# First heads of an attention kernel: order of the loads, one head's hash bits apart, values and their scale later

## The chip, the cores and the metric

One core of a Trainium2 chip runs the kernel. The metric is device time in microseconds (us), the median of timed executions. A further execution was profiled; every duration below is from it.

## The reference

Two batches of 8 heads (16 heads, sequence 768, head size 64, fp32) go through attention with a hash mask: six projections of each q and k row give six sign bits, and a query sees a key only if all six agree. The result is the input of a top-1 mixture of experts (8 experts, 1536 tokens), whose output goes through a gated two-layer network.

```python
q_bits = (einsum('bhsd,dk->bhsk', q, proj) > 0)
k_bits = (einsum('bhsd,dk->bhsk', k, proj) > 0)
mask = q_bucket[:, :, :, None] == k_bucket[:, :, None, :]
scores = where(mask, q @ k.T / sqrt(D), -1e9)
attn = exp(scores - max(scores)) ; attn /= sum(attn) + 1e-9
x = attn @ v
out = moe2(moe(x))
```

## The kernel before, in words

**Operands of a head.** q and k of head h are loaded together as the tile `r` (128 x 768: 64 rows of q, 64 of k). `prep(h)` splits it into a high and a low part (`hi`, `lo`) and SyncE's queue (SP) moves the halves into four tiles of the head's set, `X`, `K2`, `K1`, `Y`: four moves of `hi`, two of `lo`, 192 KB each. `bits(g)` makes the sign bits of the four heads 4g to 4g+3: `dot(n, i)` is the projection of head i, half n, on TensorE into 32 rows of a PSUM tile, and `rows(n)` turns half n into +-0.5 on VectorE (tile `b`). `put_bits(h)` moves head h's 12 rows of q bits to `X` and of k bits to `K2` (two DMAs on SP). Head 0 gets its bits apart, straight into its set.

**Steps.** The attention is 96 steps k, six for each head. `scores(k)` (lines 402 and 403) is one block of 128 keys against 768 queries, followed by the exponential on ScalarE (line 404); `high(k)` and `low(k)` split it into two fp16 parts (ScalarE and GpSimd, lines 412 and 418); `pv` multiplies with the values, four steps later and two steps at a time. `mx(n)` (lines 385 and 388) computes the row maxima that are needed before the scores of a head: two matmuls and two VectorE reductions for each of its six query groups; after the sixth, `top` goes by a DMA into row 76 of the head's `X`. `mx` runs ahead of the steps: `mx(0)` to `mx(5)` come before step 0, and the list `AHEAD` (from `Q['ac']`) spreads the next: before the change `mx(6)`, `mx(7)` in step 2, `mx(8)` to `mx(11)` in step 3, then one in each step. `mx(12)`, the first of head 2, is in step 4, and needs head 2's bits in place.

**Order.** The order on each engine is the program order. `at(t, f)` and `spread(t, gen, d)` put a piece of work behind a time t in steps; `due(k - 0.5)` runs before step k's scores and `due(k)` at the end of step k. `Q` holds these times: `v4` and `vg0` for the value tiles of the first heads, `lr` and `lv` for loads, `vsd` for the scale, `hn` for the number of warming matmuls (`heat`, line 283: 512 columns of zeros, result unused) before step 0 and in steps 0 to 7.

**Values.** `load_v(g)` loads the values of four heads (768 KB), `vmax` takes their largest magnitude (four reductions), and `vscale(g)` turns that into a power of two: maxima, a transpose through PSUM (`psn`, line 531), a maximum of it (line 534), a broadcast matmul (`pso`, line 540), and a chain of small integer operations (lines 544 to 559) that ends with `sc`. `vsplit` and `vgate` (line 491: twelve matmul records from the tile `vt`) need `sc`. All of `psn`, `pso`, the bits of `bits(g)` without tiles of its own and `psg` of `vgate` come from `misc`, a PSUM pool with a single buffer; a new tile in it waits until the last reader of the one before it is done.

**Before the change** the loads of heads 0 to 3, the first values and the first `vt` are queued on SP at the start; the bits of heads 0 to 3 are made together, in two PSUM tiles of their own, two dots behind `mx(5)` and six behind the warming matmuls; `put_bits(1)` and `put_bits(2)` stand in the lead-in, as does most of `vscale(0)`.

Of the kernel before, what the change touches and what calls it, by code (L numbers as in the profile page):

```python
# [51 lines left out]
def moe_attention_kernel(ctx, tc, qk, v, vt, pj, wg, w1, w2, win, wout, out, cap):  # L52
# [8 lines left out]
    def f32(t):  # L61
        return t.bitcast(F32)

    def run(gen):
        for _ in gen:
            pass
# [191 lines left out]
                )  # L258


    Q = {'v': (-3.25, -4.75, -1.75, -2.25), 'vg': (-4.5, -4.75), 'vgd': 1, 'pr': (-13.0, -12.75, -12.0, -12.5), 'prd': 0.6, 'b0': 7.75, 'b': 1.75, 'bd': 0.5, 'vm0': (8.0, 8.25, 10.75, 13.0), 'vm': (-0.5, 4.75, 7.0, 12.25), 'vs': 13.25, 'pa': 1.5, 'ev': 0.5, 'lvt': -5.0, 'v4': (2.0, 3.75, 4.0, 16.25), 'vg0': (1.85, -4.4, 7.75), 'p2': 3.5, 'lr': (0, 3, 1.5, 4.5), 'lv': 5.5, 'vsd': 0.75, 'ac': (0, 0, 2, 6, 7, 8, 9, 10), 'hd': (3, 5, 17), 'hn': (4, 4, 2, 2, 4, 3, 0, 0, 0), 'ap': (0,), 'h0': (7,), 'hl': (4,), 'l0': (), 'll': (1, 10), 'ht': (5, 9)}


    with ExitStack() as actx:
# [81 lines left out]
        def signs(out, ps, c):  # L346
            dve.tensor_scalar(out=out, in0=ps, scalar1=0.0, scalar2=c, op0=ALU.is_gt, op1=ALU.subtract)

        def bits(g, tiles=None):

            b_t[g] = ph.tile([P, S], F32R, tag="b", name=f"b{g}", bufs=2)
            ps = [None] * 2

            def dot(n, i):
                if i == 0:
                    ps[n] = tiles[n] if tiles else misc(f"psb{g}{n}")
                c = slice(n * HS, (n + 1) * HS)
                pe.matmul(
                    ps[n][32 * i : 32 * i + 32, :HS], pj_sb[:, 0:32], rt[4 * g + i][:, c], start=True, stop=True
                )  # L360

            def rows(n):
                signs(b_t[g][:, n * HS : (n + 1) * HS], ps[n][:, :HS], cst_sb[:, 0:1])

            if tiles:
                for i in range(4):
                    for n in range(2):
                        dot(n, i)
                    yield
            for n in range(2):  # L370
                if not tiles:
                    for i in range(4):
                        dot(n, i)
                    yield
                rows(n)
                if not tiles:
                    yield

        def mx(n):
            h, c = divmod(n, NC)  # L380
            st = sets[h % 4]
            mm = mxs[h % 2]
            for n in range(2):
                ps = ps_m.tile([P, 512], F32, tag="m", name=f"psm{h}{c}{n}")
                pe.matmul(  # L385
                    ps[:, :HS], st["X"][0:76, c::NC], st["K2"][0:76, n * HS : (n + 1) * HS], start=True, stop=True
                )
                dve.tensor_reduce(out=mm[:, c, n : n + 1], in_=ps[:, :HS], axis=AX.X, op=ALU.max)  # L388
            if c == NC - 1:

                dve.tensor_reduce(out=top[:, h], in_=mm, axis=AX.X, op=ALU.max)
                sp.dma_start(out=f32(st["X"])[76:77, :].rearrange("o (p c) -> o p c", c=NC), in_=f32(top)[:, h])

        def scores(k):
            h, j = divmod(k, NC)
# [108 lines left out]
                )  # L504
                yield

        def load_v(g):
            vr_t[g] = pt.tile([P, 4, NC, D], F32, tag="vr", name=f"vr{g}")
            n = 4 * NC * D
            sp.dma_start(out=vr_t[g].rearrange("p h c d -> p (h c d)"), in_=v[:, g * n : (g + 1) * n])  # L510
            am_t[g] = ph.tile([P, 4], F32, tag="am", name=f"am{g}")

        def vmax(g, i):
# [136 lines left out]
        load_r(0)  # L650
        act.dma_start(out=pj_sb, in_=pj)
        dve.memset(wg_sb, 0.0)
        for h in range(1, 4):
            load_r(h)
        load_v(0)
        load_vt(0)
        for i in range(2):
            act.dma_start(out=wg_sb[i * D : (i + 1) * D, :, i], in_=wg[i * D : (i + 1) * D])
        st, r0 = sets[0], rt[0]
# [11 lines left out]
                signs(st[t][D : D + 12, c], ps[D : D + 12, :HS], cst_sb[D : D + 12, i : i + 1])  # L671
        run(pre[0])
        next(pre[1])
        for i in range(4):
            pool.dma_start(out=f32(sets[i]["K2"])[76:77], in_=neg)
        consts()
        pool.dma_start(out=xd[0:1, :], in_=zrow[:, :DM])
        DOT = (5,)
        b0 = bits(0, [ps_v.tile([P, 512], F32, tag="v", name=f"psb0{n}") for n in range(2)])
        for n in range(NC):  # L680
            mx(n)
            if n in DOT:
                next(b0)
        heat(ps_t, "t", Q["hn"][0])
        for i in range(4):
            vmax(0, i)
        vs = vscale(0)
        next(vs)
        next(vs)
        run(b0)  # L690
        next(vs)
        put_bits(1)
        run(pre[1])
        next(pre[2])
        put_bits(2)

        heat_t.clear()
        STEPS = NC * NH
# [26 lines left out]

            at(k, part, k)

        spread(0, vs, Q["vsd"])
        spread(Q["p2"], pre[2])
        for i in range(4):  # L730
            at(Q["lr"][i], load_r, 4 + i)
# [13 lines left out]
        for h in range(NH):  # L745
            k = NC * h + NC - 1 + LAG
            if h < NH - 1:
                at(k + Q["ev"], evac, h)
            if h % 2 == 0:
                if h == 0:  # L750
                    spread(Q["vg0"][0], vgate(0), Q["vg0"][1])
                else:
                    spread(Q["vg0"][2] if h == 2 else NC * h + Q["vg"][h % 4 // 2], vgate(h // 2), Q["vgd"])
            elif h < NH - 1:
                at(k + Q["pa"], pair, h // 2)
                at(NC * h + Q["lvt"], load_vt, h // 2 + 1)
        spread(66, route(0, lambda: misc("psr0")), 1.5)
        spread(84, weigh(0))
        spread(89, any_unmatched())
# [580 lines left out]
```

## Time and profile before

| | us |
|---|---|
| timed runs | 714.74, 714.94, 719.21 (median 714.94) |
| profiled execution | 712.88 |
| its span in the trace | 711.1 |

TensorE (PE) is busy for 682.9 us of the span, VectorE (DVE) 503.5, ScalarE (ACT) 376.8, GpSimd (POOL) 260.6. The page divides the span into 40 slices with busy shares and the granted TensorE clock; the mean clock over the span is 0.98. PEld is TensorE's weight load. Matmul records of neighbouring instructions overlap, so a step's length is read from starts, not from the sum of durations.

### The profile page before, as it was taken

How to read it: one execution, taken by the hardware profiler on the slowest of the kernel's cores; microseconds unless marked ns; L12 is line 12 of the kernel's file. 1: busy time of each engine (PE TensorE's matmuls, PEld its weight loads, DVE VectorE, ACT ScalarE, POOL GpSimd, SP SyncE). 2: the span in 40 equal slices, each digit the busy share in tenths (PEclk: the TensorE clock that was granted, in tenths of full speed). 3: DMA queues.
4: the chain of work that ended last, by engine and by line, in shares of the span. 5: the costliest groups of instructions: out<-in, count | busy, mean ns of one | idle time of the engine just before them, and what ended most of it. 6: DMA issues, size and time to landing. Idle time of an engine off the chain costs nothing. (4 is left out here: it accounts for less than half of the span.)

```text
span 711.1 us, 14232 instructions
## 1 busy us (share of the span) xinstructions
PE 682.9 (96%) x5528; PEld 598.2 (84%) x5528; DVE 503.5 (71%) x988; ACT 376.8 (53%) x713; POOL 260.6 (37%) x202
## 2 busy tenths in 40 slices
PE   7999999999998699999999998999999999999996
PEld 2689898898897489999999996788888888888885
DVE  6778889889999788778777785888888632222320
ACT  3468869778779366655666642333333442223420
POOL 4347877977982411110110001333333423311212
PEclk8789999999999999999999999999999999999999
DMA  7585855746480376666665543234333000000001
GB/s 224 120 227 130 239 141 156 226 127 167 98 230 25 115 238 223 218 208 209 209 213 189 193 150 123 89 128 137 121 119 118 1 17 29 30 16 1 0 30 59
DMA packets 37841, 94.14 MB, mean 132 GB/s; under 512 B 7576, under 2 KB 13720, under 8 KB 37760
## 3 DMA queue, kind: packets, MB, share of 16 engines
q1 hardware_dynamic: 34672, 85.71, 40.2%
q0 software_dynamic: 2400, 7.36, 3.1%
q8 instruction: 46, 0.75, 0.4%
q14 instruction: 35, 0.29, 0.1%
q10 hardware_dynamic: 688, 0.03, 0.1%
HBM read 67.14 MB, written 6.29 MB: 103 GB/s over the span
## 5 line engine op out<-in xcount | busy, mean ns | idle before, releaser
L418 POOL TENSOR_TENSOR plo<-pf,phi 128x768 f16<-128x768 f32 x86 | 146.7, 1728 | 60.6 <-ACT phi L412 25.9
L996 POOL TENSOR_TENSOR ib<-wi,ia 128x512 fp32r<-128x512 f32 x32 | 50.1, 1566 | 230.1 <-ACT ia L995 230.1
L388 DVE TENSOR_REDUCE mx<-psm 128x1 f32<-128x384 f32 x192 | 96.3, 548 | 20.1 <-PE psm L385 19.8
L404 ACT ACTIVATE pf<-pst 128x384 f32<-128x384 f32 x192 | 83.4, 486 | 48.9 <-PE pst L403 47.5
L135 DVE TENSOR_TENSOR wl<-raw,wh 128x512 fp32r<-128x512 f32 x128 | 86.7, 688 | 10.2 <-ACT wh L134 3.7
L1223 ACT ACTIVATE rl<-psg,b 128x512 f32<-128x512 f32 x64 | 37.3, 582 | 94.6 <-PE psg L1221 94.5
L1221 PE MATMUL psg<-yTh,ia 128*128 128x512 f32 (+1 forms) x256 | 86.4, 338 | 0.7 <-DVE rl L1224 0.2
L1224 DVE SCALAR_TENSOR_TENSOR rl<-rl,psg 128x512 f32<-128x512 f32 x64 | 35.1, 550 | 73.3 <-ACT rl L1223 73.3
L1221 PE MATMUL psg<-yTh,ib 128*128 128x512 f32 (+1 forms) x256 | 85.9, 335 | 0.0
L1221 PE MATMUL psg<-yTl,ia 128*128 128x512 f32 (+1 forms) x256 | 85.7, 335 | 0.0
L134 ACT ACTIVATE wh<-raw 128x512 fp32r<-128x512 f32 x128 | 77.3, 623 | 2.1 <-issue 1.5
L1243 PE MATMUL pso<-cl,gh 128*128 128x512 f32 x192 | 76.7, 399 | 0.5 <-POOL cl L996 0.5
L402 PE MATMUL pst<-Y,K 128*128 128x384 f32 x192 | 75.1, 391 | 2.0 <-ACT pf L404 2.0
L1243 PE MATMUL pso<-ch,gl 128*128 128x512 f32 x192 | 75.5, 393 | 0.0
L1243 PE MATMUL pso<-ch,gh 128*128 128x512 f32 x192 | 75.5, 393 | 0.0
L412 ACT ACTIVATE phi<-pf 128x768 f16<-128x768 f32 x85 | 71.7, 844 | 1.9
L978 PE MATMUL psy<-hh,wh 128*128 128x224 f32 x256 | 71.3, 279 | 0.0
L385 PE MATMUL psm<-K,X 76*128 76x384 f32 x192 | 66.8, 429 | 4.3 <-DVE mx L388 3.5
L978 PE MATMUL psy<-hl,wh 128*128 128x224 f32 x256 | 70.2, 274 | 0.0
L978 PE MATMUL psy<-hh,wl 128*128 128x224 f32 x256 | 70.1, 274 | 0.0
L403 PE MATMUL pst<-X,K 77*128 77x384 f32 x192 | 66.2, 345 | 0.0
L432 PE MATMUL psv<-vh,plo 128*128 128x73 f16 x576 | 63.6, 196 | 1.7 <-DVE plo L418 1.7
(204 smaller groups left out, 1642.6 us busy)
## 6 DMA issues: line engine op xcount, KB each, us to landing
raw<-in_w_dram SPq DMA_DIRECT2D x64, 512.0 KB
rc<-in_win_dram SPq DMA_DIRECT2D x16, 512.0 KB
rc<-in_wout_dram SPq DMA_DIRECT2D x16, 512.0 KB
r<-in_qk_dram SPq DMA_DIRECT2D x16, 384.0 KB
K<-hi SPq DMA_DIRECT2D x31, 192.0 KB
vr<-in_v_dram SPq DMA_DIRECT2D x4, 768.0 KB
vt<-in_vt_dram SPq DMA_DIRECT2D x8, 384.0 KB
Y<-hi SPq DMA_DIRECT2D x16, 192.0 KB
```

The costliest lines, as they stand in the source:

```text
L134: act.activation(wh[e, i][:, c], r, AF.Copy)
L135: lo.tensor_tensor(out=wl[e, i][:, c], in0=r, in1=f32(wh[e, i])[:, c], op=ALU.subtract)
L385: pe.matmul(ps[:, :HS], st["X"][0:76, c::NC], st["K2"][0:76, n * HS : (n + 1) * HS], start=True, stop=True)
L388: dve.tensor_reduce(out=mm[:, c, n : n + 1], in_=ps[:, :HS], axis=AX.X, op=ALU.max)
L402: pe.matmul(ps[:, :HS], st["K1"][:, kc], st["Y"][:, qc], start=True, stop=False)
L403: pe.matmul(ps[:, :HS], st["K2"][0:77, kc], st["X"][0:77, qc], start=False, stop=True)
L404: act.activation(pf.rearrange("k (c n p) -> k c n p", c=NC, n=2)[:, :, n], ps[:, :HS].rearrange("k (p c) -> k c p", c=NC), AF.Exp, scale=0 ...
L412: act.activation(phi_t[k], pf_t[k], AF.Copy)
L418: eng.tensor_tensor(out=plo_t[k], in0=pf_t.pop(k), in1=phi_t[k], op=ALU.subtract)
L978: pe.matmul(ps, l, r, start=n == 0, stop=n == 3 * KF - 1)
L1221: pe.matmul(ps, l, x, start=n == 0, stop=n == 3 * KD - 1)
L1243: pe.matmul(po[blk][s], l, r, start=first and n == 0, stop=last and n == 2)
```

## The change

- The lead-in loads only heads 0 and 1 at first. Head 2 is queued behind head 1's first moves, head 3 behind `put_bits(1)`, the first `vt` at the end of the lead-in. The first values go on ScalarE's queue behind `mx(5)` and behind `top` of head 0, which goes on that queue too.
- `bits` takes a list of heads. Head 1's bits are made alone behind `mx(5)`, and `put_bits(1)` follows. Heads 2 and 3 follow as `bits(0, [2, 3])` from time 1.25, spaced by 0.5, through `misc`; `put_bits(2)` stands at 3.5.
- `vscale(0)` stops behind its first maxima in the lead-in and goes on from time 1.0 in spaces of 0.5.
- The low part of head 1 is made by ScalarE and GpSimd, not by VectorE (`Q['ap']`).
- `mx(6)` to `mx(11)` come two in each of the steps 1, 2 and 3. Warming matmuls: 6 in the lead-in and 2, 2, 1, 1 in steps 0 to 3, in place of 4 and 4, 2, 2, 4, 3.
- The times of loads 4 to 7, of the second values, of `vsplit`, of `vgate(0)`, of `vmax(1)` and of the second `vt` are later by 0.25 to 3.75 steps.

```diff
--- before.py
+++ after.py
@@ -258,7 +258,7 @@
                 )
 
 
-    Q = {'v': (-3.25, -4.75, -1.75, -2.25), 'vg': (-4.5, -4.75), 'vgd': 1, 'pr': (-13.0, -12.75, -12.0, -12.5), 'prd': 0.6, 'b0': 7.75, 'b': 1.75, 'bd': 0.5, 'vm0': (8.0, 8.25, 10.75, 13.0), 'vm': (-0.5, 4.75, 7.0, 12.25), 'vs': 13.25, 'pa': 1.5, 'ev': 0.5, 'lvt': -5.0, 'v4': (2.0, 3.75, 4.0, 16.25), 'vg0': (1.85, -4.4, 7.75), 'p2': 3.5, 'lr': (0, 3, 1.5, 4.5), 'lv': 5.5, 'vsd': 0.75, 'ac': (0, 0, 2, 6, 7, 8, 9, 10), 'hd': (3, 5, 17), 'hn': (4, 4, 2, 2, 4, 3, 0, 0, 0), 'ap': (0,), 'h0': (7,), 'hl': (4,), 'l0': (), 'll': (1, 10), 'ht': (5, 9)}
+    Q = {'v': (-3.25, -4.75, -1.75, -2.25), 'vg': (-4.5, -4.75), 'vgd': 1, 'pr': (-13.0, -12.75, -12.0, -12.5), 'prd': 0.6, 'b0': 7.75, 'b': 1.75, 'bd': 0.5, 'vm0': (10.25, 11.0, 11.75, 13.0), 'vm': (-0.5, 4.75, 7.0, 12.25), 'vs': 13.25, 'pa': 1.5, 'ev': 0.5, 'lvt': -5.0, 'v4': (2.75, 3.75, 4.5, 16.25), 'vg0': (2.85, -4.4, 7.75), 'p2': 3.5, 'lr': (2, 3.5, 4.5, 5.5), 'lv': 6.5, 'vsd': 0.5, 'ac': (0, 2, 4, 6, 7, 8, 9, 10), 'hd': (3, 5, 17), 'hn': (6, 2, 2, 1, 1, 0, 0, 0, 0), 'ap': (0, 1), 'h0': (7,), 'hl': (4,), 'l0': (), 'll': (1, 10), 'ht': (5, 9)}
 
 
     with ExitStack() as actx:
@@ -346,13 +346,15 @@
         def signs(out, ps, c):
             dve.tensor_scalar(out=out, in0=ps, scalar1=0.0, scalar2=c, op0=ALU.is_gt, op1=ALU.subtract)
 
-        def bits(g, tiles=None):
-
-            b_t[g] = ph.tile([P, S], F32R, tag="b", name=f"b{g}", bufs=2)
+        def bits(g, heads=range(4), tiles=None):
+
+            if g not in b_t:
+                b_t[g] = ph.tile([P, S], F32R, tag="b", name=f"b{g}", bufs=2)
+            p = slice(32 * heads[0], 32 * heads[-1] + 32)
             ps = [None] * 2
 
             def dot(n, i):
-                if i == 0:
+                if i == heads[0]:
                     ps[n] = tiles[n] if tiles else misc(f"psb{g}{n}")
                 c = slice(n * HS, (n + 1) * HS)
                 pe.matmul(
@@ -360,21 +362,19 @@
                 )
 
             def rows(n):
-                signs(b_t[g][:, n * HS : (n + 1) * HS], ps[n][:, :HS], cst_sb[:, 0:1])
-
-            if tiles:
-                for i in range(4):
-                    for n in range(2):
-                        dot(n, i)
-                    yield
+                signs(b_t[g][p, n * HS : (n + 1) * HS], ps[n][p, :HS], cst_sb[p, 0:1])
+
             for n in range(2):
-                if not tiles:
-                    for i in range(4):
-                        dot(n, i)
-                    yield
-                rows(n)
+                for i in heads:
+                    dot(n, i)
                 if not tiles:
                     yield
+                    rows(n)
+                    yield
+            if tiles:
+                yield
+                rows(0)
+                rows(1)
 
         def mx(n):
             h, c = divmod(n, NC)
@@ -389,7 +389,7 @@
             if c == NC - 1:
 
                 dve.tensor_reduce(out=top[:, h], in_=mm, axis=AX.X, op=ALU.max)
-                sp.dma_start(out=f32(st["X"])[76:77, :].rearrange("o (p c) -> o p c", c=NC), in_=f32(top)[:, h])
+                (sp if h else act).dma_start(out=f32(st["X"])[76:77, :].rearrange("o (p c) -> o p c", c=NC), in_=f32(top)[:, h])
 
         def scores(k):
             h, j = divmod(k, NC)
@@ -504,10 +504,10 @@
                 )
                 yield
 
-        def load_v(g):
+        def load_v(g, eng=sp):
             vr_t[g] = pt.tile([P, 4, NC, D], F32, tag="vr", name=f"vr{g}")
             n = 4 * NC * D
-            sp.dma_start(out=vr_t[g].rearrange("p h c d -> p (h c d)"), in_=v[:, g * n : (g + 1) * n])
+            eng.dma_start(out=vr_t[g].rearrange("p h c d -> p (h c d)"), in_=v[:, g * n : (g + 1) * n])
             am_t[g] = ph.tile([P, 4], F32, tag="am", name=f"am{g}")
 
         def vmax(g, i):
@@ -650,10 +650,7 @@
         load_r(0)
         act.dma_start(out=pj_sb, in_=pj)
         dve.memset(wg_sb, 0.0)
-        for h in range(1, 4):
-            load_r(h)
-        load_v(0)
-        load_vt(0)
+        load_r(1)
         for i in range(2):
             act.dma_start(out=wg_sb[i * D : (i + 1) * D, :, i], in_=wg[i * D : (i + 1) * D])
         st, r0 = sets[0], rt[0]
@@ -671,28 +668,26 @@
                 signs(st[t][D : D + 12, c], ps[D : D + 12, :HS], cst_sb[D : D + 12, i : i + 1])
         run(pre[0])
         next(pre[1])
+        load_r(2)
         for i in range(4):
             pool.dma_start(out=f32(sets[i]["K2"])[76:77], in_=neg)
         consts()
         pool.dma_start(out=xd[0:1, :], in_=zrow[:, :DM])
-        DOT = (5,)
-        b0 = bits(0, [ps_v.tile([P, 512], F32, tag="v", name=f"psb0{n}") for n in range(2)])
+        b0 = bits(0, [1], [ps_v.tile([P, 512], F32, tag="v", name=f"psb0{n}") for n in range(2)])
         for n in range(NC):
             mx(n)
-            if n in DOT:
-                next(b0)
+        load_v(0, act)
+        run(b0)
+        put_bits(1)
+        load_r(3)
+        run(pre[1])
         heat(ps_t, "t", Q["hn"][0])
         for i in range(4):
             vmax(0, i)
         vs = vscale(0)
         next(vs)
-        next(vs)
-        run(b0)
-        next(vs)
-        put_bits(1)
-        run(pre[1])
         next(pre[2])
-        put_bits(2)
+        load_vt(0)
 
         heat_t.clear()
         STEPS = NC * NH
@@ -725,7 +720,9 @@
 
             at(k, part, k)
 
-        spread(0, vs, Q["vsd"])
+        spread(1.0, vs, Q["vsd"])
+        spread(1.25, bits(0, [2, 3]), 0.5)
+        at(3.5, put_bits, 2)
         spread(Q["p2"], pre[2])
         for i in range(4):
             at(Q["lr"][i], load_r, 4 + i)
@@ -753,7 +750,7 @@
                     spread(Q["vg0"][2] if h == 2 else NC * h + Q["vg"][h % 4 // 2], vgate(h // 2), Q["vgd"])
             elif h < NH - 1:
                 at(k + Q["pa"], pair, h // 2)
-                at(NC * h + Q["lvt"], load_vt, h // 2 + 1)
+                at(max(4.75, NC * h + Q["lvt"]), load_vt, h // 2 + 1)
         spread(66, route(0, lambda: misc("psr0")), 1.5)
         spread(84, weigh(0))
         spread(89, any_unmatched())
```

## Rows read from the trace of the kernel before

**Rows 1.** The page: busy time of each engine, share of the span, instructions.

```profile
PE 682.9 (96%) x5528; PEld 598.2 (84%) x5528; DVE 503.5 (71%) x988; ACT 376.8 (53%) x713; POOL 260.6 (37%) x202
```

**Rows 2.** Timeline of PE, first score record of steps 0, 2, 5 (both halves), 6, 95.

```profile
19.28 0.44 PE L402 MATMUL pst<-Y,K 128*128 128x384 f32 x1
...
22.65 0.45 PE L402 MATMUL pst<-Y,K 128*128 128x384 f32 x1
...
38.44 0.52 PE L402 MATMUL pst<-Y,K 128*128 128x384 f32 x1
39.08 0.52 PE L402 MATMUL pst<-Y,K 128*128 128x384 f32 x1
...
42.12 0.42 PE L402 MATMUL pst<-Y,K 128*128 128x384 f32 x1
...
231.18 0.45 PE L402 MATMUL pst<-Y,K 128*128 128x384 f32 x1 [0.62 <-ACT pf L404]
```

**Rows 3.** Stretches: length; busy PE, PEld, DVE, ACT, POOL; clock, DMA share, GB/s.

```profile
3.50:4.00 0.50, 0.00 (x0) 0.00 (x0) 0.07 (x1) 0.07 (x1) 0.00 (x0) 1.00 1.03 393
...
17.00:18.00 1.00, 1.00 (x7) 0.28 (x7) 0.00 (x0) 0.00 (x0) 0.00 (x0) 0.68 0.00 0
...
25.00:26.00 1.00, 0.00 (x0) 0.00 (x0) 0.96 (x5) 0.36 (x1) 0.58 (x1) 1.00 0.88 211
...
27.00:28.00 1.00, 1.00 (x7) 0.72 (x6) 0.88 (x2) 0.46 (x2) 0.93 (x1) 0.94 1.02 209
...
41.00:42.00 1.00, 1.00 (x27) 1.00 (x25) 1.00 (x4) 0.91 (x2) 0.00 (x0) 0.74 1.04 234
```

**Rows 4.** Timeline of PE, 13 to 40 us: dots, warming, maxima, gates.

```profile
13.27 2.77 PE L358 MATMUL psb<-r,pj_sb 128*32 128x384 f32 x4
...
15.97 1.84 PE L283 MATMUL heatt<-idle_sb 128*128 128x512 f16 x4
...
17.85 1.50 PE L358 MATMUL psb<-r,pj_sb 128*32 128x384 f32 x12
...
26.54 0.56 PE L385 MATMUL psm<-K,X 76*128 76x384 f32 x1 [1.63 <-DVE mx L388]
...
32.65 2.57 PE L491 MATMUL psg<-wg_sb,vt 128*128 128x16 f32 x12
```

**Rows 5.** Timeline of DVE and POOL, 14 to 28 us.

```profile
14.10 1.92 DVE L514 TENSOR_REDUCE am<-vr 128x1 f32<-128x384 f32 x4
...
19.44 1.14 DVE L347 TENSOR_SCALAR b<-psb,pj_sb 128x384 fp32r<-128x384 f32 x2 [3.09 <-PE psb L358]
...
21.78 1.78 POOL L418 TENSOR_TENSOR plo<-pf,phi 128x768 f16<-128x768 f32 x1 [8.40 <-ACT phi L412]
...
22.15 1.44 DVE L548 TENSOR_SCALAR am<-am 128x2 int32<-128x2 int32 x1
...
23.93 1.65 POOL L418 TENSOR_TENSOR plo<-pf,phi 128x768 f16<-128x768 f32 x1 [0.38 <-ACT phi L412]
24.13 1.48 DVE L554 TENSOR_SCALAR sc<-ex 128x3 int32<-128x3 int32 x1
...
25.93 1.94 DVE L388 TENSOR_REDUCE mx<-psm 128x1 f32<-128x384 f32 x4
```

**Rows 6.** Timeline of the queues and of what a transfer released.

```profile
0.81 1.96 SPq L308 DMA_DIRECT2D r<-in_qk_dram  x4
...
3.93 0.84 ACT L661 ACTIVATE K<-r 64x768 fp32r<-64x768 f32 x1 [1.62 <-DMA r<-in_qk_dram]
...
6.27 0.60 SPq L326 DMA_DIRECT2D Y<-hi  x1
...
14.09 0.84 ACT L319 ACTIVATE hi<-r 128x768 fp32r<-128x768 f32 x1 [6.99 <-DMA Y<-hi]
...
21.57 0.74 SPq L344 DMA_DIRECT2D K<-b  x1
```

**Rows 7.** Line 385 in 22 to 24 us: PE's wait ahead of `mx(6)`, ns.

```profile
L385 PEldq EVENT_SEMAPHORE  x2: 51/386/722, 23.0 to 23.1; - x2
```

## The prediction

> **What bounds the kernel now.** Read the page's engine lines first [rows 1]: PE is busy for 96% of the span, the next, VectorE, for 71%. So time is won or lost only where PE stands still, runs at the low clock or does work that isn't needed. Then read the score matmuls by their starts [rows 2]. Step 6 starts at 42.12 us and step 95 at 231.18: 89 steps, 2.12 us each. Steps 0 to 6 take 42.12 - 19.28 = 22.84 us, 3.8 each, 10.1 us above that pace. All that the change touches lies ahead of step 6 or supplies it; behind step 6 the order on PE is the old one. At step 6 both orders have also done the same work (maxima 0 to 13, the products of steps 0 and 1). So I forecast one number, the start of step 6, and carry its shift through to the end.
>
> Third, the stretches [rows 3]: the granted clock rises from 1.2 to 2.4 GHz in the stretch 17 to 18, falls back in 27 to 28 and rises in 41 to 42. It fell behind a stretch (25 to 26) in which PE did nothing: `mx(7)` waited 1.63 us for VectorE [rows 4], which was busy with the scale of the values until 25.9 [rows 5]. So the slow steps 4 and 5 are partly idle time and partly half clock.
>
> **The change part by part.** Times below are starts in the changed kernel, worked from rows of before.
>
> *To step 0.* Up to the end of `mx(5)` nothing on the path changes: head 0 was already first on the queue. Then come two dots of head 1 where two of head 0 stood (2.77 us from 13.27, ending near 16.0 [rows 4]); the six others leave. Six warming matmuls follow in place of four: four at the low clock cost 1.84 us [rows 4], 0.46 each, and behind the rise near 17.6 (the stretch 17 to 18 has a mean of 0.68 [rows 3]) one costs half of that. They end near 18.2. The transpose and the six dots (1.50 us from 17.85) no longer stand here, so step 0 starts at 18.2 in place of 19.28: 1.1 us ahead. `top` goes on ScalarE's queue at the old time; the values' load, a copy and head 2's `hi` queue behind it on ScalarE, and POOL's low part of head 1 behind the copy. They have until about 20 us, so I cost them at nothing; a late `top` would delay step 0 one for one. `put_bits(1)` can start when the two dots and two sign operations (1.14 us for two [rows 5]) are done, at 16.7; with 0.85 us for its first DMA and then 2.26 from issue to landing (issued 21.57 [rows 6], the wait ends at 23.1 + 0.72 = 23.83 [rows 7]) head 1's bits are there at 19.8, in time.
>
> *Step 1.* At the full clock a step's four score records take about 0.75 us (half of twice the 0.64 between the halves of step 5 at the low clock, with a little for the exponential [rows 2]), so with two warming matmuls step 1's scores start at about 19.45 and `mx(6)` at 20.6, both ahead of before. But the maxima on VectorE now queue behind `vmax(0)`, and that waits for the values, issued only at 14.75. Head 0's load, half as large, took 3.93 - 0.81 = 3.1 us [rows 6]; the second half at the 393 GB/s that the first loads reach [rows 3] adds 1.0, so they land at 18.85. The bounds: 3.1 us (17.85), and the 7.8 us that a move behind queued loads took (issued 6.27, waited for until 14.09 [rows 6]; 22.55). I stay near the first, because little is queued by then. `vmax` takes 1.92 us [rows 5], two small maxima 0.4, the reductions of `mx(6)` and `mx(7)` 1.94 [rows 5]: VectorE is at 23.15, and the maximum of `psn` is read at 23.4.
>
> *Step 2, the first new wait.* The dots of heads 2 and 3 (half 0) take the single `misc` buffer from `psn`, so PE must wait until VectorE has read `psn`: from 22.4 to 23.45, 1.05 us idle, with step 2's scores behind it. A half of the dots costs about 0.65 (twelve records, three heads wide, in 1.50 for two halves [rows 4]). Step 2's scores start at 24.1, where before they started at 22.65: the lead of 1.1 is now a lag of 1.45, with `mx(6)` and `mx(7)` done, though, which before came later.
>
> *Steps 2 and 3, the second wait.* `mx(8)` and `mx(9)` keep VectorE until 27.3, the signs until 27.9. `pso` needs the buffer that the signs read: PE idles from 26.2 to 27.95, 1.75 us. Then `pso`, VectorE's copy of it and the dots of half 1 in turn, from 28.45. A gap of this size preceded the fall of the clock before [rows 3, 4], so I take half clock from here: dots 1.3, scores 1.28 (twice 39.08 - 38.44 [rows 2]), a warming matmul 0.46. `mx(10)` and `mx(11)` then hold VectorE from 31.9 to 33.85, `top` 0.17, the signs of half 1 0.6: 34.65.
>
> *The scale's chain* runs at 28.25 on VectorE. Before, its two larger operations took 1.44 and 1.48 us, and each ended with a POOL subtraction beside it (21.78 + 1.78 = 23.56; 23.93 + 1.65 = 25.58 [rows 5]); the whole chain took 21.96 to 26.02. Its other operations take 0.1 to 0.3 us, so free of POOL the chain takes about 1.4 us. I place it between two subtractions and take 1.4; the upper bound is 4.06. The Trainium skill (SBUF — State Buffer, "Who interferes with whom") says why: VectorE in a two-port mode and GpSimd share one port pair, and the one that comes first keeps it for its whole instruction, so the other blocks. By that rule, with which the rows agree, the chain costs 1.4 or 4.06 us according to where it falls beside POOL; the second is rival C.
>
> *Step 4, the wait that decides.* `put_bits(2)` can only start at 34.65. First DMA 0.85, second 2.26 to landing: 37.8. On PE only step 4's scores and one warming matmul (1.7 us) stand between `mx(11)` and `mx(12)`, which needs these bits. PE idles about 3 us and `mx(12)` starts at 37.8. Before, the twelve gate records (2.57 us from 32.65 [rows 4]) were done ahead of step 4; now they follow `mx(12)`.
>
> *To step 6*, at the low clock: `mx(12)` 0.66 (two records of 384 columns, as in a half of scores), the gates 2.35 (the last one's tail left out), and 3.68 from step 5's scores to step 6's, as before (42.12 - 38.44 [rows 2]: scores, `mx(13)`, products): 6.7 us. Step 6 starts at 44.5 in place of 42.12.
>
> *The rest.* Head 1's low part leaves VectorE (0.95 us there) for ScalarE and POOL, which wait at that point anyway. Loads 4 to 7 and the second values move by steps, but SP reached them only from 29 to 40 us before, so they come no later in time. Seven warming matmuls fewer (12 for 19) are in the starts above.
>
> **Sum:** 18.2 to step 0; 5.9 to step 2 (two steps of work, the values and the first wait); 13.7 to `mx(12)` (the second wait, half clock, the DMA); 6.7 to step 6: 44.5, which is +2.4 us on 42.12. On the profiled execution's 712.88 that is 715.3. The median of the runs shown lies 2.06 above that execution, so the forecast for runs is 717.3.
>
> **The rivals.**
>
> *A. The clock holds.* `mx(6)` to `mx(11)` no longer come in one block of eight matmuls paced by VectorE, and PE has work on both sides of each new wait. Then dots, scores and warming in step 3 take half, `put_bits(2)` starts 1.6 us sooner, `mx(12)` at 36.2, and the 6.7 us behind it shrink to 4.0: step 6 at 40.2, 1.9 us sooner than before, 713.0. For it: the clock stayed high from 17.6 to 27.9. Against it: in the only case that the rows show, the clock fell behind a gap of 1.63 us, and here two such come, then one of 3 to 4 us.
>
> *B. The change doesn't do what I read: no wait for the `misc` buffer,* because the old and the new tile overlap in no rows that matter. Then step 2's scores come at 23.05, step 3's near 26.2, `mx(12)` near 34.5 and step 6 at 41.2: 0.9 us sooner, 714.0. For it: no row of before shows such a wait. Against it: the pool has one buffer and the code's rule is a wait for the last reader.
>
> *C. Slower: the chain of the scale meets POOL.* One place: VectorE between `pso` and `mx(10)`. If a subtraction runs beside each of the chain's two larger operations, they take 1.44 and 1.48 as before, and the chain ends 2.6 us later (1.3 if only one is met). It passes to `mx(10)`, the signs, `put_bits(2)` and step 6: +5.0, 719.9. I place the end of POOL's third subtraction at 28.2 and the chain at 28.25, so C decides as soon as that subtraction comes 0.1 us later against the chain.
>
> **How the numbers follow.** The forecast's case has 0.50 (its own range 715.5 to 719, from the values' landing and the clock's moment); A 0.25, B 0.12, C 0.10, and 0.03 for more on either side. The best that I can build, A and B together, puts `mx(12)` near 34.5 and step 6 near 38.5: -3.6, or 711.3. C with values 0.6 us later gives +5.6, 720.5. The range is 711 to 720.5. One per cent is 7.1 us, about what a measurement of this kernel can tell from no change; none of the cases reaches it, since at most 10.1 us lie above the later pace and VectorE's own work from the values' landing to the signs (11.2 us) plus the DMA puts `mx(12)` at 33.3 or later. So: faster by over 1% 0.04, within 1% 0.93, slower by over 1% 0.03.
>
> **What would show it.** Step 0 starts near 18.2 us. PE is idle ahead of the dots of heads 2 and 3, released by the maximum of `psn`, and ahead of `pso`, released by the signs. `mx(12)` starts 3 us behind `put_bits(2)`, with PE idle ahead of it. The clock is at 1.2 GHz from about 28 us until the first products. The chain of small VectorE operations takes under 2 us. Step 6 starts near 44.5, and from there to step 95 the same 189 us as before. The forecast is wrong if PE has no gap of 2 us between steps 2 and 5, if `mx(12)` finds its bits in place, or if step 6 starts ahead of 42.1.

## The result, and the profile after

| | before | after |
|---|---|---|
| timed runs, median (lowest to highest), six each | 715.56 (714.41 to 719.21) | 723.08 (722.29 to 724.13) |
| profiled execution | 712.88 | 723.26 |
| its span | 711.1 | 721.5 |

The changed kernel is slower: ratio 1.0088, interval 1.0061 to 1.0116, or 7.5 us between the medians. The forecast was 717.3 with a range to 720.5, so the time lies outside it. Runs more than 1.5% above the fastest of their kernel are left out of the ratios, here and below.

The page's engine line answers to [rows 1]:

```profile
PE 685.7 (95%) x5517; PEld 599.2 (83%) x5517; DVE 502.5 (70%) x989; ACT 377.3 (52%) x714; POOL 261.6 (36%) x203
```

PE is still the bound. Of the 10.4 us by which the span grew, its busy time took 2.8; the rest is gaps. The timeline of PE in the changed kernel (start, length, line, tiles, and in brackets the idle time ahead with its releaser); the L402 lines answer to [rows 2], the waits to [rows 4]:

```profile
18.13 0.52 PE L402 MATMUL pst<-Y,K 128*128 128x384 f32 x1
...
20.57 0.98 PE L385 MATMUL psm<-K,X 76*128 76x384 f32 x3
22.65 0.55 PE L385 MATMUL psm<-K,X 76*128 76x384 f32 x1 [1.10 <-DVE mx L388]
...
24.23 0.94 PE L360 MATMUL psb<-r,pj_sb 128*32 128x384 f32 x4 [0.92 <-DVE am L534]
25.11 0.69 PE L402 MATMUL pst<-Y,K 128*128 128x384 f32 x1
...
30.30 0.56 PE L540 MATMUL pso<-dg,ones 2*128 2x2 f32 x2 [1.43 <-DVE b L347]
31.11 1.50 PE L360 MATMUL psb<-r,pj_sb 128*32 128x384 f32 x4 [0.25 <-DVE am L544]
32.53 0.69 PE L402 MATMUL pst<-Y,K 128*128 128x384 f32 x1
...
41.23 0.99 PE L385 MATMUL psm<-K,X 76*128 76x384 f32 x2 [4.37 <-DMA K<-b]
...
44.43 0.67 PE L402 MATMUL pst<-Y,K 128*128 128x384 f32 x1
...
48.73 0.42 PE L402 MATMUL pst<-Y,K 128*128 128x384 f32 x1
...
68.81 0.27 PE L531 MATMUL psn<-ident,am 128*1 128x128 f32 x1 [0.55 <-DVE am L523]
...
238.41 0.44 PE L402 MATMUL pst<-Y,K 128*128 128x384 f32 x1 [0.62 <-ACT pf L404]
```

Step 0 starts 1.15 us sooner than before (18.13 for 19.28), step 2 2.5 us later (25.11 for 22.65), step 6 6.6 us later (48.73 for 42.12). The lag of step 95 is 7.23 us (238.41 for 231.18): 0.5 us were added near 68.8 us, where the transpose of the second group's maxima waits for a reduction of values that the change made later; in the profile before, PE has no wait at that transpose.

The timeline of VectorE in the same stretch, which answers to [rows 5]:

```profile
19.75 1.93 DVE L514 TENSOR_REDUCE am<-vr 128x1 f32<-128x384 f32 x4 [2.96 <-DMA vr<-in_v_dram]
...
23.91 0.27 DVE L534 TENSOR_REDUCE am<-psn 2x1 f32<-2x128 f32 x1
...
27.57 1.95 DVE L388 TENSOR_REDUCE mx<-psm 128x1 f32<-128x384 f32 x4 [3.14 <-PE psm L385]
29.53 0.62 DVE L347 TENSOR_SCALAR b<-psb,pj_sb 64x384 fp32r<-64x384 f32 x1
...
31.09 0.17 DVE L548 TENSOR_SCALAR am<-am 128x2 int32<-128x2 int32 x1
...
31.80 0.17 DVE L554 TENSOR_SCALAR sc<-ex 128x3 int32<-128x3 int32 x1
```

Read it as one thread: the values land at 19.75, their reductions end at 21.7, the maxima of `mx(6)` and `mx(7)` follow, then `psn` is read (23.91), and only then may PE fill the bank (the single buffer of `misc`) with dots. The same happens a second time: signs at 29.53, `pso` at 30.30. The queue's timeline (issue and length) shows the two ends of the thread; the second pair answers to [rows 6]:

```profile
14.91 0.60 ACTq L510 DMA_DIRECT2D vr<-in_v_dram  x1
...
37.83 0.82 SPq L343 DMA_DIRECT2D X<-b  x1
38.70 0.75 SPq L344 DMA_DIRECT2D K<-b  x1
```

The stretches (length; busy time of PE, PEld, DVE, ACT, POOL; granted clock, DMA share, GB/s) answer to [rows 3]:

```profile
24.00:25.00 1.00, 0.77 (x4) 0.14 (x4) 0.33 (x2) 0.00 (x0) 0.02 (x1) 0.92 1.11 237
25.00:26.00 1.00, 1.00 (x5) 0.89 (x4) 0.00 (x0) 0.00 (x0) 0.00 (x0) 0.50 1.05 209
...
35.00:36.00 1.00, 0.82 (x4) 0.48 (x4) 1.00 (x3) 0.94 (x2) 0.00 (x0) 0.96 0.00 0
...
38.00:39.00 1.00, 0.00 (x0) 0.00 (x0) 0.79 (x1) 1.00 (x2) 0.00 (x0) 0.75 0.11 11
...
48.00:49.00 1.00, 1.00 (x18) 1.00 (x16) 1.00 (x3) 0.05 (x1) 0.82 (x1) 0.63 0.72 169
```

A mean between 0.50 and 1.00 places the change inside its stretch: the clock falls to 1.2 GHz near 24.8 us, is back at 2.4 GHz from 35.1 to 38.5, and then low again until 48.7. The two profiled executions differ by 10.4 us, 3 more than the medians. Those 3 us lie behind step 95, in code that the change leaves alone: 483.1 us (721.5 - 238.41) for 479.9 before. In the profiled executions of the runs below this rest takes 479.6 to 484.4, so the start of step 95 is the better measure; between these two kernels the medians agree with it (7.5 us for 7.23). The profiled execution of the kernel before is faster than each of its six timed runs, though, so starts compared with it come out late: in the runs below the ratios put the difference to before 0.4 to 3.5 us lower than the starts of step 95 do.

### The profile page after: what moved, and what is told of

The parts are those of the page before. It is cut to its first block, busy times and chain, and to the rows that moved or that the text cites. A ratio compares the mean times of both kernels' runs of the same rounds, so it can differ in the third digit from the quotient of the medians.

```text
span 721.5 us, 14215 instructions
## 1 busy us (share of the span) xinstructions
PE 685.7 (95%) x5517; PEld 599.2 (83%) x5517; DVE 502.5 (70%) x989; ACT 377.3 (52%) x714; POOL 261.6 (36%) x203
## 5 line engine op out<-in xcount | busy, mean ns | idle before, releaser
L402 PE MATMUL pst<-Y,K 128*128 128x384 f32 x192 | 75.9, 395 | 2.0 <-ACT pf L404 2.0
L385 PEld LDWEIGHTS psm<-K,X 76*128 76x128 f32 x192 | 53.2, 314 | 15.2 <-DVE mx L388 7.4
```

The source lines that it names most:

```text
L385: pe.matmul(ps[:, :HS], st["X"][0:76, c::NC], st["K2"][0:76, n * HS : (n + 1) * HS], start=True, stop=True)
L402: pe.matmul(ps[:, :HS], st["K1"][:, kc], st["Y"][:, qc], start=True, stop=False)
```

## The experiments

The theory: the change strings head 2's bits onto one thread (values, reductions, maxima, the single bank, signs, DMA), and `mx(12)` waits at its end. The rivals: the loss is the late values alone; the loss is the low clock. Each ratio is to the kernel before on the same chip. Edits are against the changed kernel unless another is named, and cuts in them are marked by dots. The intervals of the single edits overlap that of the changed kernel or come close to it, so what each of them does is read from the starts.

**Head 2's bits early.** The bits of heads 0 to 2 are made together behind `mx(5)`.

```diff
-        b0 = bits(0, [1], ...
+        b0 = bits(0, [0, 1, 2], ...
...
+        put_bits(2)
...
-        spread(1.25, bits(0, [2, 3]), 0.5)
-        at(3.5, put_bits, 2)
+        spread(1.25, bits(0, [3]), 0.5)
```

> The bits of heads 0 to 2 are made together behind mx(5), put_bits(2) stands at the end of the lead-in, head 3's bits alone at 1.25. Theory (head 2's bits come late, at the end of a chain of waits on VectorE and on one PSUM buffer): the 4.4 us that PE waits ahead of mx(12) go, mx(12) starts near 37 us in place of 41.2, step 6 near 44.3 in place of 48.7, the time falls by about 4.4 us on the changed kernel's 723.1, to 718.7. Rival 1 (the low clock is the loss, the wait only its occasion): the clock stays low through steps 2 to 5 and the time falls by less than 2 us. Rival 2 (the values' late landing is the loss): VectorE is as late as before in all that follows the values, and the time falls by less than 1 us.

Measured: 719.32 (718.20 to 720.37), ratio 1.0046 (1.0031 to 1.0060). Timeline of PE:

```profile
15.63 2.77 PE L360 MATMUL psb<-r,pj_sb 128*32 128x384 f32 x8 [0.63 <-DMA r<-in_qk_dram]
...
20.18 0.52 PE L402 MATMUL pst<-Y,K 128*128 128x384 f32 x1
...
37.99 0.84 PE L385 MATMUL psm<-K,X 76*128 76x384 f32 x2
...
45.37 0.67 PE L402 MATMUL pst<-Y,K 128*128 128x384 f32 x1
```

`mx(12)` finds its bits in place, and step 6 comes 3.4 us sooner than in the changed kernel, although step 0 comes 2.05 us later: the dots now wait for head 2's load, which the change had put back. Both waits for the bank are still there (0.91 and 1.43 us). Step 6 was expected at 44.3.

**The same, with head 2's load at the start.**

```diff
         load_r(1)
+        load_r(2)
...
-        load_r(2)
```

> The changed kernel with the bits of heads 0 to 2 made together and put_bits(2) in the lead-in, as tried before, and now head 2 loaded right behind head 1, so that the dots do not wait for its load. Theory: the 2.1 us that step 0 was late in that run come back, mx(12) starts near 36 us, step 6 near 43.3, the time is 717 to 717.5, about 1.5 us above the kernel before. What is left above before is the waits on the single PSUM buffer. Rival 1 (clock): no gain on that run.

Measured: 719.39 (718.23 to 731.55), ratio 1.0037 (0.9995 to 1.0078). Step 0 starts at 17.54, 2.6 us sooner than in the run before, but the first wait for the bank ends at 25.14 (25.39 there) and step 6 starts at 45.64, not at 43.3. A lead at step 0 is worth nothing as long as the thread from the values is late.

**Banks of their own for the dots of heads 2 and 3.** The two tiles come from the pool of the product tiles (`own` is a new argument of `bits`, the function that makes its tiles), and the one warming matmul of step 3 leaves.

```diff
-        spread(1.25, bits(0, [2, 3]), 0.5)
+        spread(1.25, bits(0, [2, 3], own=lambda n: ps_v.tile([P, 512], F32, tag="v", name=n + "b")), 0.5)
```

> The dots of heads 2 and 3 get PSUM tiles of their own, not the single buffer of the scale's tiles (one warming matmul fewer in step 3). Theory: PE's waits ahead of the dots and ahead of the scale's broadcast go (0.9, 1.4 and 0.3 us), step 3 starts near 30 in place of 32.5, put_bits(2) and mx(12) come 2.5 us sooner, near 38.7, step 6 near 46.2, and the time falls by 2.5 us, to 720.6. Rival 1 (clock): mx(12) moves by the idle time alone if the clock still falls at 24 us, at most 2 us. Rival 2 (values): no more than 1 us, as VectorE is bound by the values' landing.

Measured: 721.94 (717.01 to 727.33), ratio 1.0065 (1.0029 to 1.0100). Timeline of PE:

```profile
28.57 0.58 PE L540 MATMUL pso<-dg,ones 2*128 2x2 f32 x2
...
38.76 0.99 PE L385 MATMUL psm<-K,X 76*128 76x384 f32 x2 [3.65 <-DMA K<-b]
...
46.27 0.67 PE L402 MATMUL pst<-Y,K 128*128 128x384 f32 x1
```

The waits ahead of the dots and of `pso` are gone, so the sharing of the bank was their cause. Step 6 comes 2.5 us sooner; the wait for the bits stays.

**The values early.** Their load goes on SP, right behind head 2's.

```diff
         load_r(2)
+        load_v(0)
...
-        load_v(0, act)
```

> The first values are queued on SyncE behind the load of head 2, ahead of put_bits(1), not on ScalarE's queue behind mx(5). Theory: vmax starts near 16.8 in place of 19.75 and mx(6) and mx(7) are reduced as soon as PE has them, so the first wait on the PSUM buffer ends 1.5 to 2 us sooner; the other waits stay, mx(12) comes near 39.3, step 6 near 46.8, and the time falls by 2 us, to 721. Rival 2 (the values' landing is the loss): most of the 7.5 us come back, 716 to 717. Rival 1 (clock): at most the 2 us.

Measured: 721.49 (721.12 to 722.34), ratio 1.0074 (1.0052 to 1.0097). The reductions of the values start at 17.78, 2 us sooner. Timeline of PE:

```profile
23.19 1.32 PE L360 MATMUL psb<-r,pj_sb 128*32 128x384 f32 x4 [0.92 <-DVE am L534]
...
40.23 0.99 PE L385 MATMUL psm<-K,X 76*128 76x384 f32 x2 [4.38 <-DMA K<-b]
...
47.55 0.42 PE L402 MATMUL pst<-Y,K 128*128 128x384 f32 x1
```

The thread moves by about 1 us and keeps its three waits (0.92, 1.57 and 4.38 us). Step 6 comes 1.2 us sooner than in the changed kernel, step 95 only 0.2 (238.22). The late values alone are not the loss.

**Warming in the wait for the bits.** 18 warming matmuls are put into step 4.

```diff
-'hn': (6, 2, 2, 1, 1, 0, 0, 0, 0)
+'hn': (6, 2, 2, 1, 1, 18, 0, 0, 0)
```

> 18 warming matmuls are put into step 4, where PE waits for head 2's bits; nothing else. Theory: mx(12) starts where it did (41.2 us), since it waits for a transfer; the gates, step 5 and the first products behind it then run at 2.4 GHz and step 6 starts 2.5 to 3 us sooner, near 46; the time falls to about 720.3. Rival 1 (the low clock is the loss): the time falls by 5 us or more, to 718 or less. If the clock does not rise during the warming, mx(12) comes later by what is left of it (up to 3.5 us) and the time rises.

Measured: 722.69 (718.55 to 725.14), ratio 1.0083 (1.0059 to 1.0107). Timeline of PE:

```profile
38.22 5.87 PE L283 MATMUL heatv<-idle_sb 128*128 128x512 f16 x18
43.74 0.75 PE L385 MATMUL psm<-K,X 76*128 76x384 f32 x2
...
48.07 0.42 PE L402 MATMUL pst<-Y,K 128*128 128x384 f32 x1
...
51.35 0.55 PE L385 MATMUL psm<-K,X 76*128 76x384 f32 x1 [0.81 <-DVE mx L388]
```

From `mx(12)` to step 6 it is 4.33 us in place of 7.50: that much the high clock is worth there. But the warming itself ran at the low clock until 41.9, `mx(12)` comes 2.5 us later, and a wait for VectorE comes at 51.35; step 95 starts at 239.25, 0.84 us later than without it. Not all of this is the warming's: up to step 4's scores the two programs are the same, and yet the second DMA of `put_bits(2)` is issued 0.85 us later here (39.55 for 38.70). So a difference of about 1 us between the starts of two single executions tells nothing. Neither the 720.3 of the theory nor the 718 of the clock rival was met: the low clock has a price, but warming in this wait did not buy it back.

**All three undone.** Loads of head 2, the values and `vt` early on SP, bits of heads 0 to 2 and `put_bits(2)` in the lead-in, the scale from time 0; head 3's dots moved to time 4.25 (`v4` and `vg0` as before the change).

```diff
         load_r(1)
+        load_r(2)
...
-        load_r(2)
+        load_v(0)
+        load_vt(0)
...
-        spread(1.0, vs, Q["vsd"])
-        spread(1.25, bits(0, [2, 3]), 0.5)
-        at(3.5, put_bits, 2)
+        spread(0, vs, Q["vsd"])
+        spread(4.25, bits(0, [3]), 0.5)
```

> The changed kernel with the chain taken apart: head 2 is loaded right behind head 1 and the bits of heads 0 to 2 are made behind mx(5), put_bits(2) in the lead-in, head 3's bits only at 4.25; the values and the first vt are loaded on SyncE behind head 1's moves; the scale goes on from time 0, and the first value tiles come at the times of before, so that no tile of the single PSUM buffer is taken while another's reader is still due. Theory: no wait of PE on VectorE's signs, none on a transfer ahead of mx(12); step 6 starts at 33 to 37 us, the time is 6 to 9 us under the kernel before (0.991 to 0.988). Rival 1 (the low clock sets the pace): step 6 not before 40, the time within 2 us of before. Rival 3 (VectorE's work of the first steps is the bound whatever the order): step 6 between 38 and 42, the time within 0.5% of before.

Measured: 717.76 (715.87 to 724.36), ratio 0.9994 (0.9952 to 1.0036): level with the kernel before. Timeline of PE:

```profile
19.70 0.42 PE L403 MATMUL pst<-X,K 77*128 77x384 f32 x1 [1.27 <-DMA X<-top]
...
36.66 1.46 PE L360 MATMUL psb<-r,pj_sb 128*32 128x384 f32 x2 [1.32 <-issue]
...
42.33 0.83 PE L360 MATMUL psb<-r,pj_sb 128*32 128x384 f32 x2 [0.32 <-DVE b L347]
43.09 0.44 PE L402 MATMUL pst<-Y,K 128*128 128x384 f32 x1
```

Step 6 at 43.09, not at 33 to 37: a miss, and what the clock rival had forecast (step 6 not before 40, the time level). The clock was low from 27.5 to 41.2 us, about as long as in the kernel before, so this run leaves that rival standing. Three costs had not been put into the theory. Step 0's second record waited for the small DMA of `top`: issued at 14.57, while 276 to 329 GB/s of loads were moving (the stretches from 14 to 17 us), it was used only at 19.70. `mx(9)` waited 1.33 us for VectorE, which was busy with the scale's chain until 26.4. And head 3's dots, moved back, come behind 1.32 us of idle PE ahead of step 5 and 0.32 us ahead of step 6. For the 1.32 us the profile names no releaser, but VectorE reads the gates' tile `psg`, in the same bank, until 36.56.

**Two variations of it:** the maxima as before the change (`ac` begins 0, 0, 2), and the values on ScalarE's queue behind `mx(5)`.

```diff
-'ac': (0, 2, 4, 6, 7, 8, 9, 10)
+'ac': (0, 0, 2, 6, 7, 8, 9, 10)
```

> The same kernel with mx(6) to mx(11) in the steps of before (two in step 2, four in step 3). Theory: the bits are not late in either order, so the block of four pairs costs what VectorE needs for it; step 6 within 1.5 us of the other order and the time within 1.5 us. Rival 1 (clock): the block of eight paced matmuls lets the clock fall as in the kernel before, and the time is 3 us or more above the other order's.

Measured: 720.23 (716.83 to 725.24), ratio 1.0043 (1.0005 to 1.0081), span 715.6 for 716.6, step 6 at 44.27, 1.2 us later: within the theory's 1.5 at step 6, while the medians lie 2.5 us apart.

```diff
-        load_v(0)
+        load_v(0, act)
```

> The same kernel with the values loaded on ScalarE's queue behind mx(5), as the change has it. Theory: VectorE gets to vmax 2 to 3 us later, the transpose of the maxima on PE waits for it at the end of step 0, and all later steps are 2.5 to 3.5 us later than with early values. Rival 2 (the values' late landing is the whole loss of the change): 6 us or more. If the transfer is hidden: nothing.

Measured: 722.64 (718.97 to 726.65), ratio 1.0054 (1.0013 to 1.0096), step 6 at 47.29, 4.2 us later than with the early values. The intervals of the three overlap, so the times tell nothing safely apart; the starts of step 6 say that late values cost about 4 us in this version. PE waits 2.88 us ahead of `psn`, and the clock falls near 22.2 us, with the early values near 27.5, so the wait and the clock are not told apart.

**Bits and bank together:** the edits of the second and third run, with the banks of their own for head 3's dots alone.

```diff
+        load_r(2)
...
+        b0 = bits(0, [0, 1, 2], ...
...
+        spread(1.25, bits(0, [3], own=lambda n: ps_v.tile([P, 512], F32, tag="v", name=n + "b")), 0.5)
```

> The changed kernel with both: the bits of heads 0 to 2 and put_bits(2) in the lead-in with head 2 loaded behind head 1, and PSUM tiles of their own for head 3's dots. Theory (the two waits are separate and add up, 3.1 and 2.5 us at step 6 when each was taken alone): step 6 near 43.1, the time about 5.5 us under the changed kernel's, within 2 us of before. If one wait hides behind the other: step 6 at 45 or later.

Measured: 714.50 (713.34 to 717.89), ratio 0.9968 (0.9941 to 0.9994). Timeline of PE:

```profile
24.11 1.49 PE L360 MATMUL psb00b<-r,pj_sb 128*32 128x384 f32 x2
...
29.22 0.58 PE L540 MATMUL pso<-dg,ones 2*128 2x2 f32 x2
...
35.55 0.84 PE L385 MATMUL psm<-K,X 76*128 76x384 f32 x2
...
42.91 0.52 PE L402 MATMUL pst<-Y,K 128*128 128x384 f32 x1
```

All three new waits are gone, and with them the loss: step 6 is 5.8 us sooner than in the changed kernel (the profiled execution, 717.89, is the slowest of the ten). `mx(6)` now waits 0.99 us for head 1's bits, `mx(7)` still waits for VectorE (1.33 us), and the clock is low from 22.7 on (0.65 in the stretch 22.5 to 23). The stretch from 18 to 50 us, in the changed kernel and here, settles the clock rival:

```profile
18.00:50.00 32.00, 23.75 (x114) 17.41 (x112) 17.78 (x47) 12.98 (x24) 10.25 (x7) 0.68 0.62 174
...
18.00:50.00 32.00, 29.66 (x166) 22.17 (x164) 24.13 (x57) 16.70 (x31) 12.69 (x8) 0.68 0.77 198
```

The mean clock is 0.68 in both, some 20 us at 1.2 GHz, and yet 5.8 of the 6.6 us are gone. So the waits are the loss against the kernel before, and the low clock by itself is not.

**And the values early** (load on SP behind head 1's first moves, not on ScalarE's queue):

```diff
-        load_r(2)
+        load_v(0)
...
-        load_v(0, act)
```

> The same with the values loaded on SyncE behind head 1's first moves as well. Theory: the values' landing (19.7 us, against 17.8 when loaded early) is the rest, step 6 comes another 1 to 3 us sooner, 40 to 42, and the time is level with before or up to 2 us under it. Rival 1 (clock): no further gain beyond 1 us.

Measured: 711.14 (710.22 to 714.76), ratio 0.9932 (0.9905 to 0.9960). Step 0 starts at 17.98, step 2 at 22.97. Timeline of PE, then the stretch from 18 to 50 us:

```profile
37.61 0.60 PE L402 MATMUL pst<-Y,K 128*128 128x384 f32 x1
...
18.00:50.00 32.00, 30.79 (x234) 24.65 (x233) 27.49 (x66) 19.93 (x36) 17.04 (x11) 0.89 0.84 218
```

Step 6 is 5.3 us sooner than in the run before, more than the 1 to 3 expected; with the other waits in place early values gave 1.2 us. But the 5.3 us are not the values' alone: 1.65 of them are there at the second record of `mx(7)` (21.61 for 23.26), and the rest comes while the clock is high here, until 31.2, and low there, from 22.7 on.

**The scale back into the lead-in.** All loads at the start on SP as before the change, the bits of all four heads and both `put_bits` in the lead-in, and the whole of `vscale(0)` there too. `v4` and `vg0` are as before the change. Kept of it: two maxima in each of the steps 1 to 3, head 1's low part on ScalarE and GpSimd, `top` on ScalarE's queue, the warming, and the later loads and reductions of the second values.

```diff
+        b0 = bits(0, range(4), ...
...
+        for i in range(4):
+            vmax(0, i)
+        vs = vscale(0)
...
+        run(vs)
...
-        spread(1.0, vs, Q["vsd"])
-        spread(1.25, bits(0, [2, 3]), 0.5)
-        at(3.5, put_bits, 2)
```

> Loads as in the kernel before; the bits of all four heads in one group behind mx(5), put_bits(1) and put_bits(2) at once, the whole scale of the values in the lead-in (its broadcast behind the warming matmuls); of the change there remain mx(6) to mx(11) two per step from step 1, head 1's low part off VectorE, top on ScalarE's queue, the counts of warming matmuls. Theory: nothing in steps 0 to 3 waits for a chain through VectorE, the small operations of the scale run before POOL's first subtraction; step 0 near 19, step 4 near 29, step 6 between 32 and 36, the time 6 to 9 us under before (0.992 to 0.988). Rival 1 (clock): it falls near 24 to 28 us all the same, step 6 not before 38, the gain under 4 us. Rival 3 (VectorE's work bounds these steps in any order): step 6 between 38 and 42.

Measured: **710.63 (708.23 to 713.59), ratio 0.9914 (0.9888 to 0.9940)**, faster than both kernels. Timeline of PE:

```profile
19.64 0.44 PE L402 MATMUL pst<-Y,K 128*128 128x384 f32 x1
...
27.83 0.56 PE L385 MATMUL psm<-K,X 76*128 76x384 f32 x1 [0.21 <-DVE mx L388]
28.22 2.07 PE L491 MATMUL psg<-wg_sb,vt 128*128 128x16 f32 x12
...
31.56 0.84 PE L385 MATMUL psm<-K,X 76*128 76x384 f32 x2
...
36.02 0.42 PE L402 MATMUL pst<-Y,K 128*128 128x384 f32 x1
```

Step 0 is 0.36 us later than in the kernel before and 1.5 later than in the changed one, but VectorE is free of the scale from 21.25 on, and between steps 0 and 4 the timeline marks no wait of PE over 0.21 us. Step 6 is 6.1 us sooner than before, 12.7 sooner than in the changed kernel.

The same with the maxima (`ac`) and the warming of the steps 0 to 4 as before the change:

```diff
+'ac': (0, 0, 2, 6, 7, 8, 9, 10)
...
+'hn': (6, 4, 2, 2, 4, 3, 0, 0, 0)
```

> The same with mx(6) to mx(11) in the steps of before, and the warming counts of steps 0 to 4 of before. If the early maxima are the gain, step 6 comes 3 us or more later than with them and the time is within 3 us of before; if the scale and the bits in the lead-in are the gain, step 6 is within 1.5 us of the other kernel's.

Measured: 711.62 (709.00 to 713.86), ratio 0.9927 (0.9895 to 0.9960). Step 6 at 38.35: 2.3 us later than with the spread maxima, which lies between the two conditions, and 3.8 us sooner than before. The intervals of the times overlap. So the larger part of the lead at step 6 does not need the spread maxima. That it belongs to the scale in the lead-in is not shown: the run with early values came to 711.14 with the scale in the steps. These three versions (711.14, 710.63, 711.62) have a mean clock of 0.89 from 18 to 50 us, the kernel before 0.79.

## Why the prediction was wrong

| start, us | forecast | after |
|---|---|---|
| step 0 | 18.2 | 18.13 |
| `mx(6)` | 20.6 | 20.57 |
| values landed | 18.85 | 19.75 |
| first dots of heads 2 and 3 | 23.45 | 24.23 |
| step 2 | 24.1 | 25.11 |
| `pso` | 27.95 | 30.30 |
| step 3 | 29.75 | 32.53 |
| `put_bits(2)` | 34.65 | 37.83 |
| `mx(12)` | 37.8 | 41.23 |
| step 6 | 44.5 | 48.73 |

The mechanism was right in its main points: step 0 sooner, the two waits for the bank with the releasers named, the long wait of `mx(12)`, the same order behind step 6. The runs show it by taking the waits away: early bits remove the last, own banks the first two, both together the loss. What failed is the size of four terms, the moment at which the clock falls above all, and through them the sum of +2.4 us, which measured +6.6 at step 6. Of the 5.8 us between the forecast and the median, 4.2 are there at step 6 and 0.6 come behind it; another 0.6 lie in the base, since the median of all six runs before is 715.56 and that of the three shown was 714.94.

**The values' landing** ("I stay near the first, because little is queued by then") measured 4.84 us from issue to use (14.91 to 19.75), not 4.1. It put the first dots 0.8 us late. The bound of 7.8 us had been the far one; the truth lay between.

**The clock** is the largest error: "I take half clock from here", from `pso` on, near 28 us. It fell near 24.8, just behind the first wait for the bank. So the scores, the warming and the maxima of step 2 ran at 1.2 GHz too: from step 2's scores to the first reduction of `mx(8)` it is 2.46 us (25.11 to 27.57), and 1.42 at 2.4 GHz in the run with the bits, the bank and the values (22.97 to 24.39). The reductions of `mx(8)` and `mx(9)` ended at 29.52 in place of 27.3, and the lag grew from 0.8 us at the first dots to 2.35 at `pso`. Another 0.43 us came between `pso` and step 3, where half clock was in the forecast: `pso` to the dots took 0.81 for 0.5, the dots 1.42 for 1.3. The row I had, a fall behind a gap of 1.63 us, was one case; I read it as the least gap that does it. Here `mx(7)` had waited 1.10 us, which I had not counted, and the dots 0.92.

**From step 3 to the landed bits** (8.05 us forecast, 8.70 measured) the lag grew by 0.65: 0.4 until the signs, 0.25 in the DMA, whose second issue landed after 2.53 us, not 2.26. The clock came back at 35.1 us for the scores of step 4, which gained nothing: PE then waited 4.37 us.

**The last stretch** took 7.50 us in place of 6.7; 0.6 of the 0.8 lie between step 5 and step 6 (4.30 for the 3.68 before). Before, the clock rose near 41.5, 0.6 us ahead of step 6 [rows 3]; here near 48.7, together with it. I had carried the old stretch over, rise included.

**"The same 189 us as before"** behind step 6 came out as 189.68 for 189.06: 0.5 us is the transpose at 68.8 us that waits for the later `vmax(1)`. I had costed the later loads at nothing and left the later reductions out.

Of the rivals, A (the clock holds) and B (no wait for the bank) fell by the rows above. C was not met: the chain took 1.49 us (30.89 to 32.38), 0.17 us for each of the two operations that had taken 1.44 and 1.48 [rows 5]. GpSimd's subtraction had ended at 29.88, 1 us ahead of it. That was luck: I had put the two 0.05 us apart, and both came later, the subtraction by 1.7 us and the chain by 2.6. The Trainium skill (SBUF — State Buffer, "Who interferes with whom") lets VectorE wait only while GpSimd holds the port pair; this trace agrees, with 0.17 us beside nothing.

The four errors had the same sign and lay on one thread, so they added up. The range held each term's spread but not their sum: the upper end was C with 0.6 us for the values, and no case in it had a clock that falls earlier.

What decides the moment at which the clock falls stays open. So does how much of the gain of the last three versions is due to each of their edits, and how much to the clock: a mean of 0.89 from 18 to 50 us is some 7 us at 1.2 GHz, the 0.79 of the kernel before 13.

## What to carry to other kernels

A piece of work that is put back "until it is needed" should be followed to its last user through every engine and bank: here one late load, one shared bank and one DMA lay on one thread, and a lead of 1.1 us at step 0 became a lag of 6.6 us six steps later. In a pool with one buffer, two chains that take turns wait for each other's readers; count a wait for each turn, or give one of them a bank of its own. When a forecast has several terms on one thread, add their upper bounds together for the range, and price the low clock from the first gap on as one of its ends.

## What the hardware showed that I had not expected

- The clock can fall without a long wait. In the version with the scale in the lead-in it fell near 28.8 us, 0.5 us behind the start of the gates, where no wait of PE over 0.21 us is marked since step 0. Its stretch:

```profile
28.00:29.00 1.00, 1.00 (x8) 1.00 (x9) 1.00 (x3) 0.26 (x1) 0.66 (x1) 0.88 1.09 212
```

- The same instructions do not fix the clock. Up to step 4's scores the run with 18 warming matmuls is the changed kernel, and the clock rose near 28.2 us in it and fell again near 31.6; in the changed kernel's own execution it stayed low from 24.8 to 35.1.
- Warming is slow to pay: in the run with 18 warming matmuls the clock rose near 41.9 us, 3.65 us after the first of them had started.
- A small DMA issued among large loads can be late: `top`'s took 5.1 us from issue to use (14.57 to 19.70) in the run with all three undone. In the changed kernel, issued at 14.33 with 116 GB/s in the stretch from 14 to 15 us, it held up nothing at 18.49.
